# Linear-attention plus maxout feed-forward on one core: hand order, q and k turned by the DMA crossbar, attention in 64x64 array tiles

## The chip, the core and the metric

One core of a Trainium2 chip. The metric is device time of one execution in microseconds (us), on the slowest (here the only) core; lower is better. Times in this document are medians of fast runs. The profile is one execution recorded by the hardware profiler; its span (first to last instruction) is about 1.7 us shorter than the measured time.

Engine names: PE is TensorE (matmuls), PEld its weight loads, DVE is VectorE, ACT is ScalarE, POOL is GpSimd (here mostly the issuer of the loads that cast fp32 to bf16), SP is SyncE (the issuer of the output DMAs and, after the change, of the crossbar transposes; SPq is its time spent issuing them). "Turning" a matrix below means transposing it on its way to the matmul. A DMA "lands" when all its data have arrived; its landing time counts from the start of its issue.

## The reference

```python
k_proj = np.einsum('ks,bhsd->bhkd', E, k)          # E, F: 64 x 1024
v_proj = np.einsum('ks,bhsd->bhkd', F, v)          # q, k, v: 8 batches, 8 heads, 1024 tokens, 64
scores = q @ k_proj.T / sqrt(64)                   # 1024 x 64 per head
attn   = softmax(scores)
x      = attn @ v_proj                             # 8192 tokens x 512
h      = max(x @ w1, x @ w2, x @ w3)               # 512 -> 768
out    = h @ w_out                                 # 768 -> 512
```

Per batch: project k and v from 1024 tokens to 64, turn q and the projected k (the 64 head dimensions must lie on partitions for the scores), scores, exponential, AV, normalise, and then the feed-forward part, which is by far the larger share of the arithmetic.

## The kernel before

A scheduler orders the instructions. All transposes are TensorE matmuls against an identity, followed by a copy out of PSUM. Two heads at a time go through one 128-row matmul against a block-diagonal k (and v), so half of the array multiplies zeros.

```python
# projections, 64 columns of the array, k then v
nc.tensor.matmul(out=kp_ps[0:KP, ...], lhsT=eT[:, si, :], rhs=k_t[:, hs, si, :], ...)      # L108
...
# q: gather two heads, 8 transposes, one copy out, per pair of heads
nc.tensor.transpose(out=qt_ps[:, si * P:(si + 1) * P], in_=q_p2[:, si, :], identity=ident) # L141
nc.any.tensor_copy(out=qT_sb, in_=qt_ps.rearrange("a (si p) -> a si p", p=P))              # L147
nc.tensor.matmul(out=sc_ps, lhsT=kpT_bd[:, g, :], rhs=qT_sb[:, csl, :], ...)               # L154
nc.scalar.activation(out=pT_g[:, csl, :], in_=sc_ps, func=AF.Exp, scale=scale)             # L160
...
# AV with a ones column per head for the softmax sum; tokens on partitions
nc.tensor.matmul(out=av_v[:, gg, 0:2 * D + 2], lhsT=pT[g][:, si, :], rhs=vp_bd[:, g, :], ...)  # L200
nc.vector.reciprocal(...); nc.vector.tensor_tensor(out=x_sb..., op=ALU.mult)               # L209, L210
nc.tensor.transpose(out=xt_v[:, ct, 0:P], in_=x_flat[:, ct * P:(ct + 1) * P], identity=ident)  # L220
...
# feed-forward, per half batch of 512 tokens
for jt in range(NJT):                       # 6
    for i in range(3):                      # w1, w2, w3
        for ct in range(NCT):               # 4
            nc.tensor.matmul(out=h_ps[i], lhsT=w_sb[i][:, ct, ...], rhs=rhs_x[:, ct, :, :], ...)  # L237
    ...                                     # ACT copy, two DVE maxima
for tt in range(4):
    for jt in range(NJT):
        nc.tensor.matmul(out=o_ps, lhsT=hT[:, jt, ...], rhs=wout_sb[:, jt, :], ...)        # L252
```

The softmax here doesn't subtract the row's maximum and nothing guards it: scores larger than these inputs give would overflow.

## Time and profile before

| | before |
|---|---|
| time | 466.9 us (466.53 to 467.27) |
| PE busy | 431.2 us, 93% of the span |
| period of one batch in steady state | 52.8 us |
| feed-forward share of a period | 192 matmuls x 216 ns = 41.4 us |
| attention share of a period | 11.4 us |
| batch 0's attention, alone at the start | up to about 50 us |

From the page, part 1 (busy us, share of the span, instructions per engine) and part 2 (busy tenths in 40 slices of the span, granted TensorE clock in tenths, DMA share):

```profile
PE 431.2 (93%) x2623; PEld 226.4 (49%) x2672; DVE 228.9 (49%) x550; ACT 173.4 (37%) x311; POOL 54.7 (12%) x74
PE   1474999999999999999999999999999999999995
PEclk9996999999999999999999999999999999999999
DMA  8999999319620691209820592202020200202102
PE 89%; DMA 8%; issue 1%; DVE 1%; POOL 1%; ACT 0%; POOLq 0%
```

The last line is part 4, the chain of work that ended last, by engine. PE is the bound: it is on 89% of that chain and nearly always busy after the first four slices. The 16 DMA engines are full for the first seven slices (about 80 us), while everything that batches 0 to 2 and the feed-forward part need is loaded, and again for part of every later batch.

The table of stretches (start:end, then length, then busy us per engine, then granted clock, DMA share, GB/s) gives the start and one steady batch:

```profile
0.00:45.40 45.40, 20.27 (x137) 13.83 (x138) 11.80 (x41) 11.24 (x19) 15.98 (x27) 0.91 1.11 185
101.10:154.00 52.90, 52.48 (x327) 27.53 (x334) 28.75 (x69) 21.03 (x39) 6.47 (x8) 1.00 0.48 100
```

Columns after the length are PE, PEld, DVE, ACT, POOL. A steady batch leaves PE 0.4 us of rest in 52.9.

### The profile page before, as it was taken

How to read it: one execution, taken by the hardware profiler on the slowest of the kernel's cores; microseconds unless marked ns; L12 is line 12 of the kernel's file. 1: busy time of each engine (PE TensorE's matmuls, PEld its weight loads, DVE VectorE, ACT ScalarE, POOL GpSimd, SP SyncE). 2: the span in 40 equal slices, each digit the busy share in tenths (PEclk: the TensorE clock that was granted, in tenths of full speed). 3: DMA queues.
4: the chain of work that ended last, by engine and by line, in shares of the span. 5: the costliest groups of instructions: out<-in, count | busy, mean ns of one | idle time of the engine just before them, and what ended most of it. 6: DMA issues, size and time to landing. Idle time of an engine off the chain costs nothing.

```text
span 465.2 us, 6667 instructions
## 1 busy us (share of the span) xinstructions
PE 431.2 (93%) x2623; PEld 226.4 (49%) x2672; DVE 228.9 (49%) x550; ACT 173.4 (37%) x311; POOL 54.7 (12%) x74
## 2 busy tenths in 40 slices
PE   1474999999999999999999999999999999999995
PEld 1343655455544555455544555455544555444442
DVE  2025575527934375426935376425935277334351
ACT  1142555235432543235532553235432453322322
POOL 7212240004000320005000320001000000000000
PEclk9996999999999999999999999999999999999999
DMA  8999999319620691209820592202020200202102
GB/s 118 207 210 206 208 205 207 111 80 171 113 92 0 144 201 20 92 41 189 133 92 1 132 193 39 92 0 92 2 91 0 92 1 0 92 0 92 56 36 90
DMA packets 30208, 45.78 MB, mean 98 GB/s; under 512 B 1121, under 2 KB 28001, under 8 KB 28129
## 3 DMA queue, kind: packets, MB, share of 16 engines
q0 software_dynamic: 27872, 28.58, 38.2%
q1 hardware_dynamic: 2304, 16.78, 8.7%
q8 instruction: 21, 0.34, 0.3%
q14 instruction: 11, 0.08, 0.1%
HBM read 57.15 MB, written 16.78 MB: 159 GB/s over the span
## 4 chain that ended last, share of the span: by engine, by line
PE 89%; DMA 8%; issue 1%; DVE 1%; POOL 1%; ACT 0%; POOLq 0%
PE ps_m L237 53%; PE ps_m L252 18%; DMA q_t<-in_q_dram 5%; PE ps_s L220 3%; PE ps_s L154 3%; PE ps_s L200 3%; PE ps_s L108 3%; PE ps_s L141 3%; DMA k_t<-in_k_dram 2%; PE ps_s L172 2%; PE ps_s L120 0%; DVE qT_sb L147 0%; POOL q_t L101 0%; DVE x_sb L210 0%; DVE zinv L209 0%
## 5 line engine op out<-in xcount | busy, mean ns | idle before, releaser
L237 PE MATMUL ps_m<-xT,w_sb 128*128 128x512 bf16 x1109 | 263.8, 380 | 2.5 <-issue 0.7
L237 PEld LDWEIGHTS <-w_sb 128*128 128x128 bf16 x1152 | 107.5, 98 | 111.8 <-issue 3.3
L245 ACT COPY h1s<-ps_m 128x512 f32<-128x512 f32 x96 | 56.3, 586 | 105.1 <-PE ps_m L237 104.2
L252 PE MATMUL ps_m<-wout_sb,hT 128*128 128x512 bf16 x378 | 85.1, 379 | 0.2
L259 ACT COPY o_acc<-ps_m 128x512 f32<-128x512 f32 x64 | 37.5, 585 | 71.4 <-PE ps_m L252 68.9
L252 PEld LDWEIGHTS <-hT 128*128 128x128 bf16 x384 | 37.3, 98 | 45.2 <-DVE hT L248 3.5
L225 ACT COPY xT<-ps_s 128x512 bf16<-128x512 bf16 x58 | 34.1, 587 | 60.3 <-PE ps_s L220 60.2
L210 DVE TENSOR_TENSOR x_sb<-ps_s,zinv 128x256 bf16<-128x256 f32 x128 | 48.6, 417 | 0.2
L160 ACT ACTIVATE pT_g<-ps_s 128x512 bf16<-128x512 f32 x64 | 34.8, 596 | 19.9 <-PE ps_s L154 19.9
L220 PE MATMUL ps_s<-ident,x_sb 128*128 128x128 bf16 x256 | 35.4, 226 | 5.7 <-DVE x_sb L210 5.6
L220 PEld LDWEIGHTS <-x_sb 128*128 128x128 bf16 x256 | 21.8, 100 | 24.9 <-DVE x_sb L210 13.2
L101 POOL DMA_DIRECT2D k_t<-in_k_dram x16 | 12.0, 753 | 166.1 <-PE ps_s L108 162.5
L200 PE MATMUL ps_s<-vp_bd,pT_g 128*128 128x130 bf16 x256 | 30.4, 227 | 0.5 <-DVE vp_bd L185 0.5
L147 DVE COPY qT_sb<-ps_s 128x1024 bf16<-128x1024 bf16 x31 | 21.4, 691 | 17.5 <-PE ps_s L141 17.5
L108 PE MATMUL ps_s<-k_t,eT 128*64 128x256 bf16 x128 | 17.5, 291 | 10.5 <-DMA k_t<-in_k_dram 10.2
L154 PE MATMUL ps_s<-qT_sb,kpT_bd 128*128 128x512 bf16 x64 | 20.9, 410 | 3.8 <-DVE qT_sb L147 2.4
L128 DVE COPY kpT_bd<-ps_s 64x256 bf16<-64x256 bf16 x6 | 1.7, 283 | 45.2 <-PE ps_s L120 45.2
L209 DVE RECIPROCAL zinv<-ps_s 128x4 f32<-128x4 f32 x128 | 17.8, 170 | 8.3 <-PE ps_s L200 8.1
L108 PEld LDWEIGHTS <-eT 128*64 128x64 bf16 x128 | 14.2, 116 | 13.8 <-issue 12.8
L200 PEld LDWEIGHTS <-pT_g 128*128 128x128 bf16 x256 | 19.5, 101 | 2.6 <-DVE vp_bd L185 2.6
L101 POOL DMA_DIRECT2D v_t<-in_v_dram x16 | 12.0, 762 | 14.2 <-PE ps_s L172 8.2
L172 PE MATMUL ps_s<-v_t,fT 128*64 128x256 bf16 x128 | 13.2, 291 | 0.0
(321 smaller groups left out, 259.0 us busy)
## 6 DMA issues: line engine op xcount, KB each, us to landing
out_dram<-o_acc SPq DMA_DIRECT2D x16, 1024.0 KB, 3.9
q_t<-in_q_dram POOLq DMA_DIRECT2D x16, 512.0 KB, 11.4
k_t<-in_k_dram POOLq DMA_DIRECT2D x16, 512.0 KB, 8.6
v_t<-in_v_dram POOLq DMA_DIRECT2D x16, 512.0 KB, 10.7
w_sb<-in_moe_w_dram POOLq DMA_DIRECT2D x3, 768.0 KB, 22.4
wout_sb<-in_moe_w_out_dram POOLq DMA_DIRECT2D x1, 768.0 KB, 24.9
e_sb<-in_E_dram POOLq DMA_DIRECT2D x1, 128.0 KB, 3.3
f_sb<-in_F_dram POOLq DMA_DIRECT2D x1, 128.0 KB, 3.2
```

Source lines behind the costliest of these rows:

```text
L101: nc.gpsimd.dma_start(out=dst[:, hs], in_=sv[:, hs])
L108: nc.tensor.matmul(out=kp_ps[0:KP, hh * (H // 2) * D:(hh + 1) * (H // 2) * D], lhsT=eT[:, si, :], rhs=k_t[:, hs, si, :], start=(hh == 0 an ...
L154: nc.tensor.matmul(out=sc_ps, lhsT=kpT_bd[:, g, :], rhs=qT_sb[:, csl, :], start=True, stop=True,)
L160: nc.scalar.activation(out=pT_g[:, csl, :], in_=sc_ps, func=AF.Exp, scale=scale,)
L200: nc.tensor.matmul(out=av_v[:, gg, 0:2 * D + 2], lhsT=pT[g][:, si, :], rhs=vp_bd[:, g, :], start=(gg == 0), stop=(gg == 1),)
L210: nc.vector.tensor_tensor(out=x_sb[:, 4 * u:4 * (u + 1), :].rearrange("p (g par) d -> p g par d", par=2), in0=av_b[:, :, :, 0:D], in1=zinv ...
L220: nc.tensor.transpose(out=xt_v[:, ct, 0:P], in_=x_flat[:, ct * P:(ct + 1) * P], identity=ident,)
L225: nc.any.tensor_copy(out=xT[:, :, si, :], in_=xt_v[:, :, 0:P])
L237: nc.tensor.matmul(out=h_ps[i], lhsT=w_sb[i][:, ct, jt * P:(jt + 1) * P], rhs=rhs_x[:, ct, :, :], start=(ct == 0), stop=(ct == NCT - 1),)
L245: nc.scalar.copy(out=h1s, in_=h_ps[0])
L252: nc.tensor.matmul(out=o_ps, lhsT=hT[:, jt, tt * P:(tt + 1) * P], rhs=wout_sb[:, jt, :], start=(jt == 0), stop=(jt == NJT - 1),)
L259: nc.scalar.copy(out=o_acc[:, tt, :], in_=o_ps)
```

## The change

Its intent: take the transposes of q, k and x off TensorE and pack what attention work is left, so that a batch costs little more than its feed-forward matmuls.

- q (1 MB per batch) and the projected k (128 KB) are turned by DMA transposes issued from SP. Token parity goes to the two halves of the partitions, so no block-diagonal operand is needed.
- Projections of k and v use the left and the right 64 columns of the array; scores, AV and a matmul against ones (which gives the softmax sum already broadcast over partitions) use 64x64 tiles, four at a time, into four PSUM banks.
- AV now produces x already turned. The reciprocal is exp(-ln(sum)) on ACT.
- All engines run in program order; attention groups of batch b+1 are put at fixed slots between the feed-forward groups of batch b.
- HBM loads are issued by POOL as soon as their buffer is free.

```diff
+    ctx.enter_context(tc.manual_schedule())
+    def q_turn(b):
+        nc.sync.dma_start_transpose(out=qT[b % NB]..., in_=q_t[b % NB]...)
...
+        def kv(lo, hi):
+            for si in range(lo, hi):
+                nc.tensor.matmul(out=ps[0:KP, AB, :], lhsT=eT[:, si, :], rhs=k_t[i][:, :, si, :], ...)
+                nc.tensor.matmul(out=ps[KP:P, AB, :], lhsT=fT[:, si, :], rhs=v_t[i][:, :, si, :], ...)
+        def kv_out():
...
+            nc.sync.dma_start_transpose(out=kpT[i], in_=kp2[i].rearrange("p h c d -> p (h c d)"))
...
+        def scores(u):
...
+            mm(hA, 0, 0); mm(hC, 0, 1); mm(hD, 1, 0); mm(hB, 1, 1)     # (head, row half, column half)
+            mm(hB, 0, 0); mm(hD, 0, 1); mm(hC, 1, 0); mm(hA, 1, 1)
+            ... two Exp of 128 x 1024
+        def av(g):
+            for what in (0, 1):                                        # ones, then v
+                for r in range(2):
+                    for col, h in ((0, hA), (1, hB)):
+                        nc.tensor.matmul(out=ps[col * D:(col + 1) * D, AB + 2 * (1 - what) + par, :],
+                                         lhsT=ones[rows, :] if what == 0 else vp2[i][rows, h, :],
+                                         rhs=pT[rows, h, :], start=True, stop=True)
+            ... Ln, Exp(-x), one DVE multiply of 128 x 1024
+        # slots: kv 1, kv_out 3, scores(0) 10, av(0) 14, av(1) 19, scores(1) 24, av(2) 29, av(3) 34
...
+    load(0, k, k_t); load(0, v, v_t); load(0, q, q_t)     # on three lines
+    ... weight loads
+    q_turn(0)
+    for _, g in attention(0): g()
+    load(1, ...); q_turn(1)
+    for b in range(B):
+        groups = attention(b + 1) if b + 1 < B else []
+        if b + 2 < B: load(b + 2, ...)
+        ... feed-forward of batch b, groups at their slots
+        if b + 2 < B: q_turn(b + 2)
```

## The prediction

> **What bounds it.** TensorE. The chain of waits is 89% PE; in steady state PE is busy 52.3 to 52.5 us of every 52.8 at granted clock 1.00 (table of stretches). ACT (21 of 53), DVE (28.5 of 53) and DMA (0.48) have slack. Feed-forward is 192 matmuls of 512 columns per batch; the chain shows 24 in 5.18 us (216 ns each), so 41.4 us per batch, 331.5 in all, which stays. Attention is the other 11.4 us of a batch. Seven batches are interleaved so (80 us); the first runs alone: PE is busy only 20 of the first 45.4 us.
>
> **PE, per batch.** Gone: 32 q, 32 x and 4 k transposes and the 130-column AV matmuls. In their place, all 512 columns wide: 16 projections (two column tiles), 16 scores and 32 AV/ones matmuls (64x64 tiles). One after another those 64 would cost 64 x 216 ns = 13.8 us, more than now. The Trainium skill, "TensorEngine Tiling (Array Packing)", Key Properties, says that different tiles can execute weight loads and matmuls in parallel; nothing in this trace shows it. With full concurrency: 8 + 4 + 8 rounds x 216 ns = 4.3 us. The page also says that a mode change drains the array: here entering and leaving the 128*64 projection costs about 0.1 us each way (timeline), so 8 visits add about 1.6. I expect imperfect packing and 6.5 us: 5 us saved per batch, 34 over seven.
>
> **Added elsewhere.** ACT per batch: 12 activations of 1024 columns, about 1.02 us each (a 1024-column copy took 1.01), 25 us in all: fits. DVE: 24 x 0.69 + 4 multiplies of about 1.25 (from 417 ns at 256 and 693 at 512 columns), 23 us: fits. But order is fixed: after each AV group DVE stands behind Ln, Exp and multiply, about 3.5 us, while four feed-forward banks hold 4 x 0.86 = 3.4. So PE stalls up to 0.5 us in some groups; with a late k transpose, 1 to 1.5 us a batch, about 10 in all.
>
> **DMA.** q (1 MB) and k (128 KB) are turned once per batch. The skill, "DMA: Bandwidth & Descriptors", Latency and other measured facts, gives 261 GB/s for DMA transposes, 4 us for q; beside the loads I estimate 7 to 12. In steady state it hides, issued about five matmul groups before the batch ends. At the start it doesn't: at 207 GB/s k, v and q land near 20 us, q's turn shares the DMA with weight loads until 30 to 33 us, and the unhidden scores-Exp-AV-Ln-Exp-multiply chain of batch 0 takes about 19. Feed-forward starts near 52 us against 45 to 50 now: 4 us lost.
>
> **Sum.** 52 + 331.5 + 7 x 6.5 + 10 + 4 (tail) = 443; the measured time is 1.7 above the span. Predicted 444 us, 80% range 424 to 466. Faster by over 2%: 0.78; within 2%: 0.12; slower: 0.10.
>
> **What would show it.** Right: tiled matmuls of one round starting within tens of ns of each other; PE busy per batch down to 46 to 48 us; period from 52.8 to about 49.5; first feed-forward matmul at 50 to 55 us; short PE waits for DVE after AV groups. Wrong in packing: tiled matmuls 216 ns apart, or paced by weight loads (116 ns each); period 53 or more. Wrong in DMA: PE waits for a transpose at each batch's first scores matmul.
>
> **What would make it wrong.** No overlap of tiles (about 510 us) or half (about 475); q's turn far slower, stalling scores every batch; fixed-order stalls above 2 us a group; or, to the good side, full packing with no stalls (about 424).

## The result, and the profile after

| | before | changed |
|---|---|---|
| time | 466.9 us | 481.75 us (480.57 and 482.93) |
| ratio of fast runs | | 1.032, 95% interval 1.0257 to 1.0384 |
| PE busy | 431.2 us | 394.6 us |
| first feed-forward matmul | 45.4 us | 75.85 us |
| period in steady state | 52.8 us | 50.7 to 54.1, and 47.6 in the last full one |

The change is 3% slower, where 5% faster was predicted. Ratios are computed as the mean time of one kernel's fast runs over that of the other's fast runs of the same rounds, so they are not quite the ratio of the medians quoted. (The two runs of the changed kernel have recorded mean granted clocks of 0.926 and 0.993 and differ by only 2.4 us. That says little of the clock, since a recorded mean can be wrong: e4 below, with a mean of 0.993, records full clock over its first 80.5 us, yet neighbouring k matmuls of its first projection start about 0.42 us apart instead of 0.215. Where the text speaks of half clock, the spacing of the matmuls shows it too.)

The same parts of the page as shown of before:

```profile
PE 394.6 (82%) x2025; PEld 163.4 (34%) x2064; DVE 181.4 (38%) x243; ACT 197.3 (41%) x273; POOL 40.6 (8%) x60
PE   1300038699979999899979997999999999999996
PEclk9955557899988999899999998999999999999999
DMA  8999997941698046911696159815111511111122
PE 73%; DMA 16%; SPq 4%; ACT 2%; DVE 2%; POOL 1%; issue 1%; DVEq 0%; POOLq 0%
```

PE is busy 37 us less, yet the span grew. The chain has got 16% of DMA and 4% of SP's queue. The PE row shows where: three slices of nothing near the start, under a DMA row of nines, and then a dent in every batch, until the loads end; after that the row is all nines. The granted clock falls to half in the start and dips in the dents.

The table of stretches, columns as before, one line for the start and three batches of the steady state (cut at the first feed-forward matmul, and then where feed-forward resumes after the first half of a projection):

```profile
0.00:75.85 75.85, 12.35 (x81) 4.81 (x83) 6.23 (x9) 14.42 (x15) 18.33 (x30) 0.66 1.15 188
127.54:181.64 54.10, 50.19 (x253) 20.38 (x257) 22.52 (x30) 24.45 (x34) 4.46 (x6) 0.94 0.58 119
234.10:284.77 50.67, 47.43 (x254) 19.73 (x257) 22.52 (x30) 24.45 (x34) 4.45 (x6) 1.00 0.62 128
336.85:384.47 47.62, 47.35 (x254) 19.75 (x257) 22.52 (x30) 24.45 (x34) 0.00 (x0) 1.00 0.23 70
```

The last line is the first batch in which POOL issues no loads (its column is 0.00). There the period is 47.62 us with PE busy 47.35: attention costs 47.6 - 41.4 = 6.2 us of a batch instead of 11.4. That is the packed case of the prediction, and it is there, in the trace: in the projection the two column tiles start within 10 ns of one another, a pair every 215 ns (timeline; start us, length us, engine, line):

```profile
126.80 0.38 PE L88 MATMUL ps<-k_t,eT 128*64 128x512 bf16 x1
126.80 0.38 PE L90 MATMUL ps<-v_t,fT 128*64 128x512 bf16 x1
127.01 0.38 PE L88 MATMUL ps<-k_t,eT 128*64 128x512 bf16 x1
127.01 0.38 PE L90 MATMUL ps<-v_t,fT 128*64 128x512 bf16 x1
158.81 0.63 PE L113 MATMUL ps<-qT,kpT 64*64 64x512 bf16 x8
```

The last line is a whole scores group: eight matmuls of 512 columns in 0.63 us. So the Trainium skill's "TensorEngine Tiling (Array Packing)", Key Properties (tiles operate independently), agrees with this trace. Packing is not where the time went. The list of waits (engine, line, waited for: us in total, times, longest us) names one large wait of PE:

```profile
PE ps L113 <- DMA kpT<-kp: 54.3, 6, 38.0
PE ps L88 <- DMA k_t<-in_k_dram: 6.1, 1, 6.1
PE ps L156 <- DVE hT L163: 0.3, 1, 0.3
```

PE waits 54.3 us for k's turn at the first scores of a batch (L113): 38.0 at batch 0, and 3.0 to 3.8 at each of five more. The second line is the wait for the first load of k; every kernel here has such a wait at the start. The stalls that I had expected of the fixed order (the third line) are 0.3 us in all. SP's own timeline gives the issue time of each turn:

```profile
21.91 19.61 SPq L74 DMA_TRANSPOSE qT<-q_t  x1
41.58 6.36 SPq L99 DMA_TRANSPOSE kpT<-kp  x1
59.45 18.28 SPq L74 DMA_TRANSPOSE qT<-q_t  x1
131.82 1.51 SPq L99 DMA_TRANSPOSE kpT<-kp  x1
175.87 4.81 SPq L74 DMA_TRANSPOSE qT<-q_t  x1
```

Batch 0's q turn keeps SP for 19.6 us before SP even gets to k's turn behind it; it lands 33.0 us after its issue. In steady state the same instruction takes 4.8 us to issue and lands after 6.4. And k's turn of 131.82 landed 9.1 us later, where its fastest took 2.5. POOL's timeline shows what began just before it:

```profile
130.72 1.48 POOL L71 DMA_DIRECT2D k_t<-in_k_dram  x2 [44.07 <-PE ps L90]
```

POOL had waited 44 us for PE's last projection matmul (L90), which frees the k buffer. The finished projection thus releases two things at once: the copies from which k's turn is made, and 3 MB of loads, of which the first 1 MB is issued before the turn. The 9.1 us have two parts. The turn's first packet ran at 136.18, 4.4 us after its issue, behind some 600 load packets (without loads, at 341.09, it ran after 1.2 us). Then its packets took 4.3 us, about one for each load packet (434 to 440 between 137 and 140 us; 0.9 us without loads). The second part is explained under e6; why the first packet waits so long no run here shows. PE then stands for 3.5 us, and the granted clock in the 5.3 us behind that wait (140.90 to 146.20) is 0.50.

The clock falls behind some of these waits and not behind others, and the length of the wait doesn't decide it: by the spacing of the matmuls too, it fell behind 3.04 us here and 2.95 in e3, and stayed at 1.00 behind 2.98 here (the batch of 234.10) and 3.39 in e4. That the moment counts agrees with the free-running window in "TensorE: Matmul & The Clock Gate", Part 1. The page's length of about 3.4 us doesn't fit as well, since waits of 2.95 and 3.04 us are shorter.

### The profile page after: what moved, and what is told of

It reads as the page before. It is cut to its first block, busy times and chain, and to the rows that moved or that the text cites. A ratio compares the mean times of both kernels' runs of the same rounds, so it can differ in the third digit from the quotient of the medians.

```text
span 481.2 us, 5204 instructions
## 1 busy us (share of the span) xinstructions
PE 394.6 (82%) x2025; PEld 163.4 (34%) x2064; DVE 181.4 (38%) x243; ACT 197.3 (41%) x273; POOL 40.6 (8%) x60
## 4 chain that ended last, share of the span: by engine, by line
PE 73%; DMA 16%; SPq 4%; ACT 2%; DVE 2%; POOL 1%; issue 1%; DVEq 0%; POOLq 0%
PE ps L156 49%; PE ps L168 16%; DMA kpT<-kp 13%; SPq L74 4%; PE ps L130 4%; DMA q_t<-in_q_dram 3%; PE ps L88 3%; PE ps L113 2%; ACT pT L118 1%; DVE xT L136 1%; DVE kp L98 1%; ACT kp L97 1%; ACT rinv L135 0%; ACT lns L134 0%; POOL v_t L71 0%
## 5 line engine op out<-in xcount | busy, mean ns | idle before, releaser
L156 PE MATMUL ps<-xT,w_sb 128*128 128x512 bf16 x1127 | 269.2, 385 | 2.0 <-issue 0.5
L161 DVE TENSOR_TENSOR m<-ps,h1s 128x512 f32<-128x512 f32 x96 | 66.2, 690 | 114.7 <-PE ps L156 114.4
L168 PE MATMUL ps<-wo_sb,hT 128*128 128x512 bf16 x370 | 94.1, 385 | 0.7
L159 ACT COPY h1s<-ps 128x512 f32<-128x512 f32 x96 | 56.1, 584 | 61.8 <-PE ps L156 61.8
L136 DVE TENSOR_TENSOR xT<-ps,rinv 128x1024 bf16<-128x1024 f32 x32 | 39.2, 1225 | 109.5 <-ACT rinv L135 109.5
L163 DVE TENSOR_TENSOR hT<-ps,m 128x512 bf16<-128x512 f32 x96 | 66.3, 691 | 35.5 <-PE ps L156 27.6
L170 ACT COPY o_acc<-ps 128x512 f32<-128x512 f32 x64 | 37.4, 584 | 75.0 <-PE ps L168 74.8
L118 ACT ACTIVATE pT<-ps 128x1024 bf16<-128x1024 f32 x32 | 31.0, 1021 | 68.4 <-PE ps L113 68.4
L113 PE MATMUL ps<-qT,kpT 64*64 64x512 bf16 x128 | 12.2, 462 | 55.7 <-DMA kpT<-kp 54.3
L134 ACT ACTIVATE lns<-ps 128x1024 f32<-128x1024 f32 x32 | 32.8, 1024 | 25.5 <-PE ps L130 25.5
L135 ACT ACTIVATE rinv<-lns 128x1024 f32<-128x1024 f32 x32 | 33.8, 1057 | 1.0
L113 PEld LDWEIGHTS <-kpT 64*64 64x64 bf16 x128 | 2.6, 112 | 63.4 <-DMA kpT<-kp 57.7
L88 PE MATMUL ps<-k_t,eT 128*64 128x512 bf16 x64 | 19.1, 427 | 6.1 <-DMA k_t<-in_k_dram 6.1
L90 PE MATMUL ps<-v_t,fT 128*64 128x512 bf16 x64 | 18.9, 427 | 4.4 <-DMA v_t<-in_v_dram 4.4
```

Source lines behind the costliest of these rows:

```text
L88: nc.tensor.matmul(out=ps[0:KP, AB, :], lhsT=eT[:, si, :], rhs=k_t[i][:, :, si, :], start=(si == 0), stop=(si == SI - 1))
L118: nc.scalar.activation(out=pT[:, 4 * u + 2 * h2:4 * u + 2 * h2 + 2, :], in_=ps[:, AB + 2 * h2:AB + 2 * h2 + 2, :], func=AF.Exp, scale=scale)
L134: nc.scalar.activation(out=lns[n2], in_=ps[:, AB + 2:AB + 4, :], func=AF.Ln)
L135: nc.scalar.activation(out=rinv[n2], in_=lns[n2], func=AF.Exp, scale=-1.0)
L136: nc.vector.tensor_tensor(out=xT[b % 3][:, g, :, :], in0=ps[:, AB:AB + 2, :], in1=rinv[n2].rearrange("p (c n) -> p c n", c=2), op=ALU.mult)
L156: nc.tensor.matmul(out=ps[:, bank, :], lhsT=w_sb[i][:, ct, jt * P:(jt + 1) * P], rhs=xT[b % 3][:, ct, ch, :], start=(ct == 0), stop=(ct == ...
```

## The experiments

Theories on trial:

- **A.** The crossbar turns are slow because they share the DMA engines with the HBM loads. At the start the loads are the weights and batch 1; in steady state the loads released by the very projection whose result is to be turned.
- **B.** A turn takes that long by itself (first use, or small k turns), whatever runs beside it.
- **C.** The fixed order of the engines makes the stalls.
- **D.** Packing brings less than it seems.

Each run was correct and is compared with the kernel before on the same chip in 3 rounds (before: 466.79 to 467.13 us there). A first group of four ran on one chip, the rest in two later groups.

| run | what it is | median us | ratio to before |
|---|---|---|---|
| changed | the change | 481.75 | 1.032 |
| e1_hold_next | loads of batch b+2 held until batch b+1 is turned | 459.47 | 0.985 |
| e2_k_pe | k turned on TensorE | 458.34 | 0.982 |
| e3_hold_start | weights and batch 1 held until batch 0 is turned | 490.3 | 1.052 |
| e4_no_pack | tile order meant to undo packing | 489.37 | 1.049 |
| e5_start_k_pe_hold | batch 0's q, every k on TensorE; loads held | 433.76 | 0.929 |
| e6_start_k_pe | the same, loads not held | 459.33 | 0.984 |
| e7_all_pe | no crossbar at all | 446.85 | 0.956 |
| e8_double | e2 with scores and AV matmuls issued twice | 480.07 | 1.028 |
| e9_best | batch 0 on TensorE, crossbar for the rest, loads held | 427.8 | 0.917 |
| e10_half_packets | e6 with load packets of half the size | 450.88 | 0.966 |

### e1: hold the next loads

```diff
+    def hold_loads(b):                                 # POOL reads a corner of both turned tiles
+        nc.gpsimd.tensor_copy(out=hold[0:1, 0:1], in_=qT[b % NB][0:1, 0, 0, 0:1])
+        nc.gpsimd.tensor_copy(out=hold[0:1, 1:2], in_=kpT[b % NB][0:1, 0, 0:1])
...
-        if b + 2 < B: load(b + 2, ...)
+        def next_loads(b=b): hold_loads(b + 1); load(b + 2, ...)
+        groups.insert(3, (10, next_loads))
```

> The changed kernel, but the loads of the batch after next wait until the next batch's q and k have been turned. Theory A (the crossbar turns are held up by the HBM loads that run beside them; the finished projection frees the k buffer and so starts the loads in the very moment k's turn is issued): k's turn lands in 2 to 3 us in every steady batch instead of 8.6, the PE wait of about 3.5 us before the first scores of a batch and the low clock behind it go, periods of 50.7 to 54.1 us become about 47.6 (as in the two batches of the changed kernel that have no loads beside them). About 20 us less in steady state, some 4 more at batch 1: 455 to 460 us. Rival B (a crossbar turn of k takes 8 to 9 us whatever runs beside it, or the fixed order on ACT and DVE makes the stall): periods stay at 50 to 54, total stays at 476 to 484.

Measured: 459.47 us, 22.3 less than the changed kernel. The landing of k's turn (first line the changed kernel, second line e1) and the only wait of PE for it (third line, at batch 0):

```profile
DMA to landing us min/median/max: 2.5/8.6/16.8
DMA to landing us min/median/max: 2.7/2.7/16.9
PE ps L118 <- DMA kpT<-kp: 38.0, 1, 38.0
```

The median falls from 8.6 to 2.7 us, and every later period is 47.6 us. Theory A holds for the steady state, and B and C fall there: the same turn is fast and the same order of engines has no stall.

### e2: k on TensorE

```diff
-            nc.sync.dma_start_transpose(out=kpT[i], in_=kp2[i]...)
+        def k_turn():
+            for h in range(H):
+                nc.tensor.transpose(out=psb[:, AB + 1, h * KP:(h + 1) * KP], in_=kp2[i][:, h, :, :], ...)
+            nc.vector.tensor_copy(out=kpT[i]..., in_=psb[:, AB + 1, :H * KP])
+        groups.append((6, k_turn))
```

> The changed kernel with k turned on TensorE (8 transposes of 64x128 and one DVE copy of 512 columns, six slots into the batch), q still by crossbar, loads where they were. If the wait before scores is for k's turn alone (A and its variant B1, slow turn), it goes: periods about 48.4 us (47.6 plus 8 transposes at about 80 ns), batch 0 starts its scores when q's turn lands, near 55 us instead of 58.4. Total 455 to 463. If the stall belongs to the fixed order of the engines or to q's turn (rival C), another wait takes its place and the periods stay above 50, total 475 or more.

Measured: 458.34 us, periods of 48.06 us. Batch 0's scores now start at 55.24 us, when q's turn lands, and no other wait took the place of the one removed. In total, taking k off the crossbar is worth as much as taking the loads out of its way: it costs 0.45 us of PE per batch (48.06 against 47.6), and feed-forward starts 3.9 us earlier (72.28 us against 76.16 in e1).

### e3: hold the loads at the start

```diff
-    ... weight loads                                   (before q_turn(0))
+    for n, (_, g) in enumerate(attention(0)):
+        g()
+        if n == 1:                                     # after k's turn was issued
+            hold_loads(0)
+            ... weight loads
```

> The changed kernel with the feed-forward weights and batch 1's loads held until batch 0's q and k have been turned. Theory A: q's turn lands 6 to 8 us after issue (near 29) instead of 33, k's within 3 to 4 instead of 16.8, first feed-forward matmul near 49 to 52 us instead of 75.9. But the held loads then run into batch 1's turns, so much of it is given back at batch 1: total 460 to 478. Rival B (the first turn is slow by itself: 19.6 us of issue on the queue that has nothing to do with loads): the turn still takes about 20 us to issue, first feed-forward matmul at 65 us or later and total above 480.

Measured: 490.3 us, outside the range: slower than the change. The part about the turn came out as theory A has it (SP's timeline):

```profile
21.94 4.81 SPq L79 DMA_TRANSPOSE qT<-q_t  x1
26.81 1.30 SPq L104 DMA_TRANSPOSE kpT<-kp  x1
64.66 20.19 SPq L79 DMA_TRANSPOSE qT<-q_t  x1
84.89 3.24 SPq L104 DMA_TRANSPOSE kpT<-kp  x1
```

The same first turn now issues in 4.81 us instead of 19.61 and lands after 6.9 instead of 33.0; the first feed-forward matmul comes at 46.77 instead of 75.85. That rules out B at the start. But the 29 us were given back, and more: the held loads now run beside batch 1's turn (third line, 20.19 us of issue, landing after 32.0), PE waits 25.5 us at batch 1's scores, and before that 4.9 and 4.5 us for batch 1's k and v, which come later. I had underrated how much a turn loses beside loads. Moving the loads without looking where they go just moves the collision.

### e4: an order meant to undo the packing

```diff
-            for si in ...: matmul(k, left columns); matmul(v, right columns)
+            for si in ...: matmul(k, left columns)
+            for si in ...: matmul(v, right columns)
-            mm(hA, 0, 0); mm(hC, 0, 1); mm(hD, 1, 0); mm(hB, 1, 1) ...
+            mm(hA, 0, 0); mm(hB, 0, 0); mm(hC, 0, 1); mm(hD, 0, 1) ...      # AV likewise: tile by tile
```

> The changed kernel with the same matmuls in an order in which neighbours mostly use the same tile of the array, so that they cannot run together (all k projections then all v ones; scores and AV matmuls of one tile back to back). Theory: packing works and is worth 44 to 50 of the 64 attention matmuls of a batch, at 216 ns: about 9 us more per batch, 60 to 75 in all, so 540 to 557 us. If packing brings little (rival D: that would be why the change lost), the time stays within 10 us of 482.

Measured: 489.37 us instead of 540 or more. By the expectation as written, packing would bring little. The trace says otherwise: the edit did not undo it. In program order this kernel issues four k projections and then four v projections (the program built from it has this order too), yet they run as pairs (timeline; L88 is k, L91 is v):

```profile
238.69 0.40 PE L88 MATMUL ps<-k_t,eT 128*64 128x512 bf16 x1
238.70 0.40 PE L91 MATMUL ps<-v_t,fT 128*64 128x512 bf16 x1
238.93 0.38 PE L88 MATMUL ps<-k_t,eT 128*64 128x512 bf16 x1
238.94 0.38 PE L91 MATMUL ps<-v_t,fT 128*64 128x512 bf16 x1
```

The fifth matmul in program order (first v) starts 10 ns after the first, and 230 ns before the second. So the experiment could not tell D from the theory, and a test that doesn't lean on order was needed (e8). Of the 7.6 us that it is slower than the change, 4.7 are before the first feed-forward matmul (80.51 against 75.85 us). The last full period, with no loads beside it, is 47.92 us against 47.62, so some 2 us more lie in the periods; the rest I did not trace.

### e8: double the packed matmuls

```diff
+            for again in range(2):
                 mm(hA, 0, 0); ... mm(hA, 1, 1)
-            for what in (0, 1):
+            for what in (0, 0, 1, 1):
```

> The kernel with k on TensorE (458.3 us), with each of the 48 scores, ones and AV matmuls of a batch issued twice (same results). Measures what these matmuls cost. Packed four to a round of 216 ns they add 12 x 0.216 = 2.6 us per batch, 18 in steady state and some 4 to 6 in batch 0 at low clock: 478 to 484 us. Two to a round: about 500. One after another: 530 or more.

Measured: 480.07 us, 21.7 more than e2 for 8 x 48 = 384 further matmuls of 512 columns: 57 ns each, where one alone in the full array takes 216. In the steady periods (50.63 against 48.06 us) it is 54 ns, a quarter of 216. They run four at a time. D falls.

### e5, e6 and e7: start on TensorE, with and without the hold, and no crossbar

e6 turns batch 0's q on TensorE, which has nothing else to do then, and every k:

```diff
-    q_turn(0)
+    for n in range(4):
+        for j in range(8):
+            nc.tensor.transpose(out=psb[:, n, j * P:(j + 1) * P], in_=q_t[0][:, h, 2 * sp:2 * sp + 2, :], ...)
+        ... copy to qT[0], DVE and ACT in turn
```

e5 is e6 with the hold of e1 (on q's turn alone), e7 turns every batch's q in this way at slots 4, 5, 7 and 8 and has no crossbar transposes.

> Three undoings together: batch 0's q and every batch's k turned on TensorE, batches 1 to 7's q by crossbar, and the loads of the batch after next held until the next q has been turned. Theory A: no crossbar turn is then beside saturated loads except batch 1's. Batch 0's scores start near 28 us, the first feed-forward matmul comes at 44 to 47 us (72.3 in the run with only k on TensorE), and the rest is as in that run: 430 to 440 us. If the start were bound by something else (weights landing, the scores-Exp-AV chain of batch 0), first feed-forward matmul at 55 or later and 443 or more.

> The same without holding the loads back: batch 0's q and every k on TensorE. Batch 1's q turn then has the loads of batches 1 and 2 beside it. Theory A: it lands some 16 to 20 us after issue instead of 6 to 8, PE waits 5 to 10 us at batch 1's scores, and the total is 4 to 9 us above the run with the loads held, 436 to 446. If contention matters only for the small k turn, it is equal to that run within 2 us.

> No crossbar at all: every q and k turned on TensorE (32 + 8 transposes per batch, as the kernel before did it), packing and hand order kept. Isolates packing and order from the crossbar. About 2.5 to 3 us more PE per batch than with q by crossbar: 448 to 456 us, with no long PE wait anywhere after the start. If the crossbar is worth having once the contention is out of the way, this is 12 to 20 us slower than the run with the loads held; if it is not, they are within 5 us.

Measured: e5 433.76, e6 459.33, e7 446.85 us. e5 is inside its range; its first feed-forward matmul comes at 47.42 us, half a microsecond late; the projections stand behind q's transposes in its order (e9 has them in front). e7 is 1 us better than expected, with a period of 49.85 us. e6 missed by 13 us: it starts as early as e5 (47.20 us) but batch 1's q turn lands 30.9 us after issue, not 16 to 20, and PE waits 24.2 us for it. Its total is that of e2 within 1 us: the 25 us won at the start were lost one batch later. Only the hold makes them stay; with it that turn lands in 6.8 us. The wait of PE in e6:

```profile
PE ps L118 <- DMA qT<-q_t: 24.2, 1, 24.2
```

The DMA records of e6, while that turn runs, say why it is so slow (queue: packets, MB, share of the 16 engines; 5 us, 68.5 to 73.5; q0 holds the loads, q1 the turn):

```profile
q0 software_dynamic: 783, 0.78, 91.9%
q1 hardware_dynamic: 781, 0.20, 30.0%
```

One packet for one packet. The turn's packets are 254 bytes (1.05 MB in 4128), the loads' about 1000, so the turn gets a fifth of the bytes. At 783 pairs in 5 us, 4128 pairs take 26 us, and before them the turn waited 4.0 us for its first packet. The pace is even: from 58.5 to 78.5 us, each 5 us move 781 to 785 turn packets. So the turn didn't wait for the loads to drain. (Here both end near 84 us; in e10 the loads go on after the turn.) That an engine goes round its queues in turn is what the Trainium skill says in "DMA: Bandwidth & Descriptors", SWDGE vs HWDGE vs iDMA; this trace agrees.

### e10: smaller load packets

To test that share (theory S in the expectation: one packet of each queue in turn), e6 with the loads of batches 1 to 7 cut so that each packet writes 512 bytes:

```diff
-            nc.gpsimd.dma_start(out=dst[b % NB][:, hs], in_=sv[:, hs])
+            for sh in range(2):
+                ss = slice(sh * SI // 2, (sh + 1) * SI // 2)
+                nc.gpsimd.dma_start(out=dst[b % NB][:, hs, ss, :], in_=sv[:, hs, ss, :])
```

> The run with batch 0's q and every k on TensorE and no hold (459.3 us; batch 1's q turn took 30.9 us beside loads), with the loads of batches 1 to 7 cut so that their packets are 512 bytes instead of 1 KB. Theory S (the 16 DMA engines take one packet of each queue in turn: the records of the middle of that turn show 783 load packets and 785 turn packets in each 5 us): pair time falls from about 6.3 ns (5.1 for the load packet, 1.2 for the turn packet) to 3.8 to 4.5 ns, 4128 pairs take 16 to 19 us, the turn lands 17 to 21 us after issue, the PE wait falls from 24 to 9 to 14 us, total 445 to 452. Rival (bytes are shared, or the turn is served when the loads have drained): the turn lands after 28 us or more, total within 4 us of 459.

Measured: 450.88 us, inside the range of theory S. The turn lands 21.6 us after issue (30.9 before) and PE waits 15.7 us, both just past the upper end of what was expected. In 8 us of that turn (58 to 66) the queues moved:

```profile
q0 software_dynamic: 2053, 1.02, 92.4%
q1 hardware_dynamic: 1792, 0.46, 42.8%
```

That is 224 turn packets per us instead of 156. There are only 0.87 per load packet because the window begins before the turn's first packet (58.56 us); from 59 to 66 us it is 1705 to 1706. Halving the other side's packets makes the turn faster by 1.4 times without touching the turn, and the loads still run when the turn is done (75.68 us). Sharing by bytes and draining are ruled out.

### e9: put together

```diff
+        if b == 0: k and q on TensorE (projections, k, q, in this order)
+        if b > 0: k by crossbar as in the change
-    ... load of the down-projection weights at the start
+        def next_loads(b=b):
+            hold_loads(b + 1)                           # on q's and k's turn
+            if b == 0: load of the down-projection weights
+            load(b + 2, ...)
```

> Batch 0 alone turned on TensorE (projections first, then k, then q), batches 1 to 7 by crossbar as in the change (q and k), loads of the batch after next, and the down-projection weights, held until batch 1's turns have landed. If the only fault of the change was that its turns ran beside loads, k by crossbar is now the cheaper way in steady state (period 47.6 against the 48.06 us with k on TensorE), and the first feed-forward matmul comes near 43 to 44 us, with a wait of 2 to 5 us at batch 1's scores because its q lands only near 50: 426 to 432 us, under the 433.8 of the run with k on TensorE. If holding loads costs the later batches their inputs, or the down-projection weights come too late, 434 or more.

Measured: 427.8 us (427.45 to 428.31), ratio 0.9165 to the kernel before (0.9141 to 0.9189). First feed-forward matmul at 43.24 us; 1.15 us of wait for k's turn at batch 1; k's turns land in 2.7 to 2.9 us, q's in 6.9 to 8.8; the steady periods are 47.62 us. It beats both kernels, with the crossbar in use for seven of eight batches.

## Why the prediction was wrong

It said 444 us; 481.75 was measured, 38 more and outside the range. Point by point, in its own order:

1. **PE per batch: right.** "I expect imperfect packing and 6.5 us": 6.2 us in the batch without loads. Of that, 4.3 are the packed rounds, so the eight visits cost 1.9 us together, near the 1.6 estimated from the trace before. e8 shows the packing by itself.
2. **Fixed-order stalls: the wrong cause.** "1 to 1.5 us a batch, about 10 in all" was meant for ACT and DVE standing behind Ln, Exp and multiply. That stall measured 0.3 us in all. (The estimate had the DVE chain right: from the start of Ln to the end of the multiply one took 3.4 us, 148.86 to 152.22. In that time PE ran a down-projection group, whose banks ACT empties and not DVE; that this is what covers the chain is read from the timeline and not tested.) In its place stood the term named only in passing, "with a late k transpose": it cost 24 us. That is 18.9 us over four periods against 47.6 (54.1, 52.46, 50.67 and 52.08), and 5.3 at batch 1 (from the first feed-forward matmul to the next projection, 50.7 us against 45.4 in e1, where that wait is gone). PE's own wait is 3.0 to 3.8 us each time, 16.3 of the 24. The half clock behind it accounts for the rest as far as the trace shows: in the one batch whose clock stayed at 1.00 (234.10 to 284.77) the excess of 3.05 us is just its wait of 2.98.
3. **The start: the step that failed most.** "q's turn shares the DMA with weight loads until 30 to 33 us", and then k's turn at once. q's turn landed at 54.9, 22 us after the predicted 33: its first packet ran 4 us after its issue, and from then on 4196 turn packets went with 4197 load packets of over four times their size. k's turn, which the prediction did not price at all, stood behind it in SP's queue until 41.58 and landed at 58.4, 3.5 us more. The first feed-forward matmul came at 75.85, not 52: 24 us. The chain of batch 0 behind it took 17.4 us (58.4 to 75.85; predicted about 19), so that step was right.
4. **In steady state "it hides".** True for q (6.4 us to landing, no wait of PE for it) and false for k. I had put q's turn in its place in time, but did not ask what the finished projection releases besides the copies: the POOL queue was waiting on that same matmul to start 3 MB of loads. The prediction had named the sign itself, "PE waits for a transpose at each batch's first scores matmul"; the trace has it in batches 0 to 5.

In numbers: 24 more at the start, 24 of k's turn in place of the stalls of 10, and 2 less for the packed work (6.2 against 6.5, seven times) make 36 of the 38 us. The remaining 2 I did not trace.

Why that is the cause and not only a story: taking away the loads beside the turn takes away the loss wherever it was done (e1 for k in steady state, e3 for q at batch 0, e5 against e6 for q at batch 1), and wherever loads were put beside a turn the loss came back (e3, e6); making the packets beside it smaller made it smaller (e10). The DMA rate quoted in the prediction, 261 GB/s, was not the fault by itself: with no loads beside it q's turn landed in 6.2 to 8.8 us in these runs, which the estimate of "7 to 12" would have covered. What failed was the price of the contention. The "7 to 12" is about what an even share of the bytes would give (an estimate: 1.05 MB at half of the 196 GB/s that the queues moved in e6 takes 11 us); the turn got a fifth. The prediction does not say how it came to the figure.

The crossbar is worth having: e5 against e7, same start, is 13 us for q; and e9 shows k on it is cheaper as well once it is alone (periods of 47.62 us against 48.06 in e5).

## What to carry to other kernels

When work moves from a full engine to DMA, price it beside the transfers that will run at the same moment: count packets, not bytes, since in these runs a stream of small packets beside one of large packets got a packet for a packet (1705 to 1706 in e10), and add the wait for its first packet (about 4 us here). Ask of each finished step everything that it releases: a freed buffer starts a load, and that load may get in front of the small transfer on which the next step waits. A hold (one tiny instruction on the loading queue that reads the result of the small transfer) cost nothing that can be seen (periods of 47.6 us with it) and was worth 22 us here; and a start that has no overlap should use the engine that is idle, in this case TensorE.

## What the Trainium skill lacked or had wrong

- "DMA: Bandwidth & Descriptors", Rules for kernel authors, says that a transpose next to ordinary DMAs needs nothing. For correctness this agrees (all runs were correct). In time it doesn't: the same 1.05 MB turn landed in 6.8 us alone and in 30.9 us beside loads (e5 and e6), and its issue kept SP for 19.6 instead of 4.8 us.
- The same page, SWDGE vs HWDGE vs iDMA, has the turn-taking of an engine's queues, packet by packet, but not what follows for unequal packets: 781 packets of 254 bytes against 783 of about 1000 in 5 us; with loads in 512-byte packets the turn landed in 21.6 us. Nor does it have the wait for the first packet behind a busy queue: 3.9 to 4.4 us after issue beside loads here, 1.2 to 1.9 without.
- The same page, Latency and other measured facts, gives 261 GB/s for DMA transposes. Here 1.05 MB from SBUF to SBUF took 6.8 us from issue to landing, 154 GB/s. Without the start-up it moved 215 GB/s (e5, 55.0 to 59.4 us).
- "TensorE: Matmul & The Clock Gate", Part 3, says that matmuls keep program order in start and end. In e4 the fifth matmul in program order started 10 ns after the first and 230 ns before the second, and it goes to another column tile. So the order in which tiles are named need not be interleaved by hand for tiles to overlap, at least within eight matmuls; e4's order cost 0.3 us a period.
- "TensorEngine Tiling (Array Packing)", Key Properties, says that a mode change drains the array but gives no cost: here 6.2 - 4.3 = 1.9 us for eight visits to a tiled mode, about 0.24 us each for going in and out, if all of the rest is put down to it.
